# Attention, two feed-forward layers and routing in one kernel: P times v in one block, one inversion for several row sums, elu with two ScalarE passes, later transposes of gathered rows

## The chip, the cores and the metric

The kernel runs on one NeuronCore of one Trainium2 chip, as a single program. The metric is the device time of one execution in microseconds (us). Five engines take part: TensorE (PE; its weight loads are shown as PEld), VectorE (DVE), ScalarE (ACT), GpSimd (POOL) and SyncE (SP), which issues most DMAs.

## The reference

Causal attention for 4 x 12 heads over 448 positions of 64 dimensions, then a dense layer with elu on 1792 tokens of 768 values, then a layer of 8 experts, to which a greedy assignment with a capacity of 224 tokens each sends every token.

```python
scores = scale * np.matmul(q, k.transpose(0, 1, 3, 2))
scores = np.where(mask, -1e9, scores); scores -= np.max(scores, axis=-1, keepdims=True)
attn = np.exp(scores); attn = attn / (np.sum(attn, axis=-1, keepdims=True) + 1e-09)
x = np.matmul(attn, v)                     # -> [1792, 768]
h = x @ w_in                               # w_in [768, 2048]
g = np.where(h > 0.0, h, np.exp(np.minimum(h, 0.0)) - 1.0)
x2 = g @ w_out                             # w_out [2048, 768]
logits = x2 @ w_gate                       # 8 experts, greedy by sorted logit, 224 tokens each
out[mask_e] = np.maximum(x2[mask_e] @ w1[e], 0.0) @ w2[e]
```

## The kernel before

Everything is unrolled in Python. Stages are generators that emit instructions and yield the PE time that they think they used; `Sched.drive` always continues the generator that is furthest behind its weight, and `after(d, fn)` puts work of the other engines on a heap, to be emitted when the emitted PE time has moved on by `d` ns. `need(token)` empties the heap up to one item. The order on every engine is the order of emission, and each engine works through its queue strictly in that order.

Attention goes by pairs of heads, n = 0 to 23. `front(n)` makes the scores of a pair in seven blocks, i = 6 down to 0, of 64 query rows for two heads (128 partitions) and 64 (i + 1) columns: one fp32 matmul (line 200), a DVE pass that adds the mask and takes the row maximum (208), an ACT exponential with the row sum (212), and, after every second block, `recip`: add 1e-9 and invert the sums of two blocks on DVE (219, 220). `norm` then scales each block on POOL (227). Where a block's width isn't a multiple of 128, POOL zeroes the last 64 columns each time (204). `back(n)` transposes the blocks (248), ACT or DVE evacuates them into `PT` (251), and P times v runs as four chunks of key rows c = 0 to 3, each for both heads of the pair, a = 0 and 1, in the two column halves of the array (262): chunks of 448, 320, 192 and 64 columns, the last with 64 key rows. Between the chunks the generator yields, so that other generators' matmuls come in between. `att(n)` runs `front(n + 1)` and `back(n)` side by side.

For n = 0 to 5 attention runs alone; the outputs of six pairs are one batch of 448 tokens. Then batch b of the dense layer (`gemm1`: 16 column tiles m, six steps of three f32r matmuls, lines 377 to 379, with high and low parts of x and of the weights) runs beside the attention of batch b + 1. In this stage DVE also converts weights that were loaded in another format, and `fold` prepares w_out and its product with w_gate. elu of a tile stands at the end of `gemm1`: ACT takes exp of the PSUM tile (389), DVE makes min(e, 1) - 1 (390), and DVE adds max(p, 0) (393).

`gemm2` (line 629, 14 token tiles of 16 steps with six matmuls) runs beside `route`, the assignment. In its last tile the rows of expert 0 that are already in DRAM are gathered (`first_rows`: two indirect DMAs on POOL, line 663, from step 4 on), and transposed in three parts by matmuls with the identity (671) after steps 11, 12 and 13; the rows of the last tile come in by a one-hot matmul (678). The table `FIRST` says at which step how many parts are emitted. Then the experts follow one after the other.

Of the kernel before, what the change touches and what calls it, by code (L numbers as in the profile page):

```python
# [8 lines left out]
F32 = mybir.dt.float32  # L9
# [5 lines left out]
AF = mybir.ActivationFunctionType  # L15
AX = mybir.AxisListType
OP = mybir.AluOpType
# [19 lines left out]
class Sched:  # L37
# [6 lines left out]
    def after(self, d, fn):  # L44
        self.n += 1
        tok = [False]
        heapq.heappush(self.heap, (self.now + d, self.n, fn, tok))
        return tok
# [28 lines left out]
def body(ctx, tc, q, k, v, w_in, w_out, w_gate, w1, w2, out, dbg=None):  # L77
# [48 lines left out]


    KN, VN, WIN, STG = {}, {}, {}, {}

# [7 lines left out]
    def load_v(n):  # L137
        b, j = divmod(n, NP)
        VN[n] = at.tile([128, 4, 2, D], F32, name="vn", bufs=3)
        SP.dma_start(VN[n][:, 0:3], v[b, j, 0:384].rearrange("(t p) h d -> p t h d", p=128))  # L140
        SP.dma_start(VN[n][:64, 3], v[b, j, 384:])


# [49 lines left out]
    def front(n):  # L193
# [3 lines left out]
        for i in range(NQ - 1, -1, -1):  # L197
            w = 64 * (i + 1)
            p = ps.tile([128, 512], F32, name="h" if n < NP and i % 2 else "sc")
            PE.matmul(p[:, :w], qT[:, i].rearrange("p a c -> p (a c)"), kT[:, :w], start=True, stop=True)  # L200
            nb = (i + 2) // 2
            s = at.tile([128, 128 * nb], F32, name=f"s{nb}", bufs=2 if nb == 4 else 4)
            if i % 2 == 0:
                G.memset(s[:, w:w + 64], 0.0)
            t0 = 1.7 * w + 250
# [10 lines left out]

            def recip(i=i, w=w):
                j = min(i + 2, NQ)
                V.tensor_scalar_add(sm[:, 2, i:j], sm[:, 1, i:j], 1e-9)
                V.reciprocal(sm[:, 2, i:j], sm[:, 2, i:j])  # L220
                for u in range(j - 1, i - 1, -1):
                    after(400, lambda u=u: norm(u))
# [8 lines left out]
            after(t0 + 1.1 * w + 350, expo)  # L231
            if i % 2 == 0:
                after(t0 + 2.0 * w + 900, recip)
# [3 lines left out]
    def back(n):  # L237
# [21 lines left out]
        for c in range(4):  # L259
            kk = min(128, S - 128 * c)  # L260
            for a in range(2):
                PE.matmul(p[64 * a:64 * a + 64, 128 * c:S], vn[:kk, c, a, :], PT[:kk, c, a, 128 * c:],  # L262
                          start=(c == 0), stop=(c == 3), skip_group_check=True)
            yield 2 * (0.835 * (S - 128 * c) + 27)
        xs = x1 if n // NP % 2 else x0
# [99 lines left out]
    def gemm1(b):  # L365
# [3 lines left out]
        for m in range(MT):  # L369
# [18 lines left out]
            g = wk.tile([128, S], F32, name="g", bufs=5)  # L388
            after(100, lambda e=e, p=p: A.activation(e, p[:, :S], AF.Exp))
            after(700, lambda e=e: V.tensor_scalar(e, e, 1.0, -1.0, op0=OP.min, op1=OP.add))  # L390

            def fin(e=e, p=p, g=g, m=m):
                V.scalar_tensor_tensor(g, p[:, :S], 0.0, e, op0=OP.max, op1=OP.add)
                SP.dma_start(gT_d[:, m, b * S:(b + 1) * S], g)
# [55 lines left out]
    for t in qz:  # L450
        G.memset(t[64:, :, 0], 0.0)
        G.memset(t[:64, :, 1], 0.0)
    G.iota(jp, pattern=[[1, 128]], base=0, channel_multiplier=-1, allow_small_or_imprecise_dtypes=True)
    V.memset(mask, 0.0)
    V.tensor_scalar(ident, jp, 0.0, None, op0=OP.is_equal)
# [136 lines left out]
    def gemm2():  # L592
        load_g(2)
        for c in range(NT):
            p = [ps.tile([128, 512], F32, name=n) for n in ("h", "tp")]
            for m in range(MT):
                if c == 0 and m == 1:
                    yield from late()
                if c == 1 and m == 0:
                    z = gb.tile([128, DM], F32, name="x2", bufs=2)  # L600
                    V.memset(z[:1], 0.0)
                    SP.dma_start(x2_d[LAST:LAST + 1], z[:1])
                if c == NT - 1 and m == 3:
                    while 0 not in IDX:
                        yield -200
                    fg = first_rows()
                if c == NT - 1 and m in FIRST:
                    for _ in range(FIRST[m]):
                        yield next(fg)
# [34 lines left out]
            X2[0] = after(300, ev), o  # L644
        for _ in fg:
            yield 0

    X2, PX, SLOT = {}, [], {}  # L650
    FIRST = {4: 1, 12: 1, 13: 1, 14: 1}

# [392 lines left out]
```

## Time and profile before

| what | value |
|---|---|
| median of 3 runs | 1059.11 us (1058.39 to 1059.22) |
| the profiled execution | 1060.71 us, span of its instructions 1058.9 us |
| PE busy | 1027.9 us, 97% |
| DVE, ACT, POOL busy | 679.4 (64%), 440.6 (42%), 246.7 us (23%) |
| mean granted clock of PE | 0.995 |

A row of the windows view gives, for a stretch of the span, its length and the busy time and number of instructions of each engine, then the granted share of PE's clock, the DMA share and GB/s. A row of the timeline has start, duration, engine, line, operation, out<-in, shape and count of merged instructions; in brackets stands the idle time of the engine just before it and what ended it. Matmuls are pipelined, so durations overlap: the next start says how long PE was really held. A row of the groups view has the count, then busy time in us, the mean of one in ns, and the idle time before them with what ended it.

### The profile page before, as it was taken

Reading aid. Unit: us, or ns where it says so; the run is one execution under the profiler, and the core shown is the slowest. Engines: PE = TensorE matmul, PEld = TensorE weight load, DVE = VectorE, ACT = ScalarE, POOL = GpSimd, SP = SyncE. Lnnn points to the kernel's source line nnn. Section 1 sums busy time; section 2 is a strip of 40 time slices with the busy share of each in tenths; the row PEclk is TensorE's granted clock in tenths of the full one; section 3 lists DMA queues with packets and bytes.
Section 4 is the critical chain, followed back from the end, with each engine's and each line's share of the span. In section 5 each row is a group of like instructions: output and inputs, shape, how many; then the busy total and the mean of one; then the engine's idle time right before and its main releaser. Section 6 shows DMA issues by size and latency. Waiting matters only on the chain.

```text
span 1058.9 us, 17901 instructions
## 1 busy us (share of the span) xinstructions
PE 1027.9 (97%) x6615; PEld 866.4 (82%) x6615; DVE 679.4 (64%) x1691; ACT 440.6 (42%) x960; POOL 246.7 (23%) x375
## 2 busy tenths in 40 slices
PE   8999998999999999999999999999989999999997
PEld 4567776667777776887898988999989999999997
DVE  5989976786854454555766565665536766667762
ACT  5655445434444454333212111111335656556651
POOL 4356563444444443000000000000020111101110
PEclk9999999999999999999999999999999999999999
DMA  7546644665522111765333333222247786676810
GB/s 182 140 147 188 211 157 144 197 198 193 186 67 88 62 38 43 245 202 159 105 105 114 122 94 96 75 72 75 77 155 228 229 258 223 209 243 229 256 32 27
DMA packets 110857, 155.32 MB, mean 147 GB/s; under 512 B 29617, under 2 KB 82353, under 8 KB 110770
## 3 DMA queue, kind: packets, MB, share of 16 engines
q1 hardware_dynamic: 108210, 143.17, 42.9%
q0 software_dynamic: 2560, 11.01, 3.5%
q8 instruction: 52, 0.85, 0.3%
q14 instruction: 35, 0.29, 0.1%
HBM read 122.17 MB, written 31.98 MB: 146 GB/s over the span
## 4 chain that ended last, share of the span: by engine, by line
PE 80%; DVE 11%; ACT 3%; issue 3%; DMA 2%; POOL 1%; SPq 0%; POOLq 0%; DVEq 0%; ACTq 0%
PE h L629 9%; PE tp L629 8%; PE h L934 8%; PE h L377 7%; PE sc L986 6%; PE h L379 6%; PE h L378 6%; PE sc L200 5%; PE pv L262 4%; PE h L931 4%; PE pv L986 3%; PE lg L986 3%; PE tp L248 3%; PE lg L768 2%; ACT s L212 1%
## 5 line engine op out<-in xcount | busy, mean ns | idle before, releaser
L377 PE MATMUL h<-xh,wh 128*128 128x448 f32 x384 | 174.4, 454 | 0.0
L505 DVE TENSOR_TENSOR wl<-wr,wh 128x768 fp32r<-128x768 f32 x144 | 135.4, 953 | 17.5 <-ACT wh L504 17.2
L212 ACT ACTIVATE s<-s,sm 128x448 f32<-128x448 f32 (+6 forms) x168 | 85.1, 507 | 138.5 <-DVE sm L208 137.1
L379 PE MATMUL h<-xh,wl 128*128 128x448 f32 x384 | 140.7, 367 | 0.0
L378 PE MATMUL h<-xl,wh 128*128 128x448 f32 x384 | 140.3, 365 | 0.0
L504 ACT CAST wh<-wr 128x768 fp32r<-128x768 f32 x144 | 118.3, 829 | 30.2 <-PE lg L986 23.4
L227 POOL TENSOR_SCALAR s<-s,sm 128x448 f32<-128x448 f32 (+6 forms) x168 | 98.1, 596 | 111.9 <-DVE sm L220 79.3
L934 PE MATMUL h<-xt,wh 128*128 128x448 f32 x384 | 119.2, 373 | 0.0
L362 POOL TENSOR_TENSOR wl<-wr,wh 128x768 fp32r<-128x768 f32 x48 | 92.1, 1918 | 103.7 <-ACT wh L361 97.6
L639 ACT COPY x<-h 128x384 f32<-128x384 f32 x14 | 6.7, 481 | 235.7 <-PE h L629 235.7
L377 PEld LDWEIGHTS h<-xh,wh 128*128 128x128 f32 x384 | 72.5, 189 | 38.0 <-issue 29.5
L208 DVE CUSTOM_DVE_ANT_0 s<-sc,mask 128x448 f32<-128x448 f32 (+6 forms) x150 | 62.1, 420 | 63.7 <-PE sc L200 58.1
L200 PE MATMUL sc<-kT,qz 128*128 128x192 f32 (+6 forms) x300 | 92.2, 395 | 1.4 <-DVE sm L208 0.5
L931 PE MATMUL h<-xt,wl 128*128 128x224 f32 x384 | 92.1, 267 | 0.0
L629 PE MATMUL h<-wh,gh 128*128 128x384 f32 x224 | 81.5, 364 | 0.0
L378 PEld LDWEIGHTS h<-xl,wh 128*128 128x128 f32 x384 | 72.9, 190 | 8.8 <-issue 3.0
L629 PE MATMUL h<-wl,gh 128*128 128x384 f32 x224 | 77.4, 346 | 0.0
L379 PEld LDWEIGHTS h<-xh,wl 128*128 128x128 f32 x384 | 72.3, 188 | 6.1
L629 PE MATMUL h<-wh,gl 128*128 128x384 f32 x224 | 76.7, 343 | 0.0
L629 PE MATMUL tp<-wh,gl 128*128 128x384 f32 x224 | 75.5, 337 | 0.0
L629 PE MATMUL tp<-wh,gh 128*128 128x384 f32 x224 | 75.4, 336 | 0.0
L629 PE MATMUL tp<-wl,gh 128*128 128x384 f32 x224 | 75.3, 336 | 0.0
(208 smaller groups left out, 2117.5 us busy)
## 6 DMA issues: line engine op xcount, KB each, us to landing
wr<-in_moe_w_dram SPq DMA_DIRECT2D x128, 384.0 KB, 3.9
gT_d<-g SPq DMA_DIRECT2D x64, 224.0 KB, 2.0
gr<-gT_d SPq DMA_DIRECT2D x28, 512.0 KB, 3.8
st<-in_moe_w_in_dram SPq DMA_DIRECT2D x16, 767.6 KB, 4.6
st<-in_moe_w_out_dram SPq DMA_DIRECT2D x16, 767.6 KB, 4.8
wo_d<-wo SPq DMA_DIRECT2D x16, 384.0 KB, 3.0
wr<-wo_d SPq DMA_DIRECT2D x16, 384.0 KB, 3.6
qz<-in_q_dram SPq DMA_DIRECT2D x48, 112.0 KB, 3.6
```

Of the source, the lines that this page charges most:

```text
L200: PE.matmul(p[:, :w], qT[:, i].rearrange("p a c -> p (a c)"), kT[:, :w], start=True, stop=True)
L212: A.activation(s[:, :w], s[:, :w], AF.Exp, bias=sm[:, 0, i:i + 1], scale=-1.0, accum_out=sm[:, 1, i:i + 1])
L227: G.tensor_scalar(s[:, :w], s[:, :w], sm[:, 2, i:i + 1], 1.0, op0=OP.mult, op1=OP.mult)
L377: PE.matmul(p[:, :S], wh[:, c], xh, start=(c == 0), stop=False)
L378: PE.matmul(p[:, :S], wh[:, c], xl, start=False, stop=False)
L379: PE.matmul(p[:, :S], wl[:, c], xh, start=False, stop=(c == KT - 1))
L504: A.copy(wh, raw)
L505: return wh, wl, after(gap, lambda: e.tensor_sub(wl, raw, wh.bitcast(F32)))
L629: PE.matmul(p[n][:, :384], st[:, mm], wsel[:, 384 * n:384 * n + 384], start=(m == 0 and first), stop=(m == MT - 1 and st is gl))
L931: PE.matmul(p[:, :CAP], wl[:, c], xt[:, c, :CAP], start=False, stop=stop, skip_group_check=True)
L934: PE.matmul(p[:, :2 * CAP], wh[:, c], xt[:, c], start=(c == 0), stop=(c == KT - 1), skip_group_check=True)
L986: PE.matmul(acc[j][n][:HC, :384], ht[:, m, s, j * HC:(j + 1) * HC], wsel[:, 384 * n:384 * n + 384], start=(m == 0 and first), stop=(m == F ...
```

## The change

P times v: all eight matmuls of a pair are emitted before the generator yields once (1980 ns); the last chunk uses 128 key rows, with v's missing 64 rows zeroed by a POOL memset at each load. The blocks of P get tiles of their own, two for each i, whose padding is zeroed once at the start; the memset for each block goes. `recip` is called after blocks 4 and 0 only, for blocks 6 to 4 and 3 to 0. elu becomes relu(-p) on ACT, exp(-that) on ACT, and max(e - 1, p) on DVE. In `gemm2`, `FIRST` moves the three parts of the transposes: two after steps 13 and 14, the third behind the last step; the wait for the index list moves from step 3 to step 4, and the generator's own times are passed on.

```diff
+    PB = [[at.tile([128, 128 * ((i + 2) // 2)], F32, name=f"s{i}{k}", bufs=1) for k in range(2)] for i in range(NQ)]
@@ load_v
         SP.dma_start(VN[n][:64, 3], v[b, j, 384:])
+        G.memset(VN[n][64:, 3], 0.0)
@@ front
-            nb = (i + 2) // 2
-            s = at.tile([128, 128 * nb], F32, name=f"s{nb}", bufs=2 if nb == 4 else 4)
-            if i % 2 == 0:
-                G.memset(s[:, w:w + 64], 0.0)
+            s = PB[i][n % 2]
-            def recip(i=i, w=w):
-                j = min(i + 2, NQ)
+            def recip(i=i):
+                j = NQ if i else 4
                 V.tensor_scalar_add(sm[:, 2, i:j], sm[:, 1, i:j], 1e-9)
                 V.reciprocal(sm[:, 2, i:j], sm[:, 2, i:j])
-            if i % 2 == 0:
+            if i in (4, 0):
                 after(t0 + 2.0 * w + 900, recip)
@@ back
         for c in range(4):
-            kk = min(128, S - 128 * c)
             for a in range(2):
-                PE.matmul(p[64 * a:64 * a + 64, 128 * c:S], vn[:kk, c, a, :], PT[:kk, c, a, 128 * c:],
+                PE.matmul(p[64 * a:64 * a + 64, 128 * c:S], vn[:, c, a, :], PT[:, c, a, 128 * c:],
                           start=(c == 0), stop=(c == 3), skip_group_check=True)
-            yield 2 * (0.835 * (S - 128 * c) + 27)
+        yield 1980
@@ gemm1
-            after(100, lambda e=e, p=p: A.activation(e, p[:, :S], AF.Exp))
-            after(700, lambda e=e: V.tensor_scalar(e, e, 1.0, -1.0, op0=OP.min, op1=OP.add))
+            after(100, lambda e=e, p=p: A.activation(e, p[:, :S], AF.Relu, scale=-1.0))
+            after(600, lambda e=e: A.activation(e, e, AF.Exp, scale=-1.0))
             def fin(e=e, p=p, g=g, m=m):
-                V.scalar_tensor_tensor(g, p[:, :S], 0.0, e, op0=OP.max, op1=OP.add)
+                V.scalar_tensor_tensor(g, e, -1.0, p[:, :S], op0=OP.add, op1=OP.max)
@@ start
+    for i in range(0, NQ, 2):
+        for t in PB[i]:
+            G.memset(t[:, 64 * (i + 1):], 0.0)
@@ gemm2
-                if c == NT - 1 and m == 3:
-                    while 0 not in IDX:
-                        yield -200
-                    fg = first_rows()
                 if c == NT - 1 and m in FIRST:
+                    if m == 4:
+                        while 0 not in IDX:
+                            yield -200
+                        fg = first_rows()
                     for _ in range(FIRST[m]):
                         yield next(fg)
@@ after the last tile
-        for _ in fg:
-            yield 0
+        for c in fg:
+            yield c
-    FIRST = {4: 1, 12: 1, 13: 1, 14: 1}
+    FIRST = {4: 1, 14: 1, 15: 1}
```

## Rows read from the trace of the kernel before

**Rows 1.** Windows of three attention stages: busy time and count of each engine, clock.
```profile
15.20:66.00 50.80, 47.25 (x268) 27.38 (x268) 39.67 (x163) 33.73 (x108) 24.23 (x64) 1.00 0.55 140
66.00:315.00 249.00, 239.66 (x1444) 176.20 (x1442) 192.80 (x500) 115.43 (x303) 122.22 (x159) 0.99 0.53 172
315.00:435.00 120.00, 120.00 (x659) 89.02 (x658) 57.13 (x181) 55.20 (x135) 47.20 (x74) 1.00 0.21 67
```

**Rows 2.** Timeline of PE in the fused stage: line, operation, tiles, shape, count.
```profile
300.94 0.60 PE L248 MATMUL tp<-ident,s 128*128 128x128 f32 x4
301.47 0.63 PE L313 MATMUL tp<-woT,wg 128*32 128x128 f32 x12
...
302.34 0.36 PE L378 MATMUL h<-xl,wh 128*128 128x448 f32 x1
302.54 0.37 PE L379 MATMUL h<-xh,wl 128*128 128x448 f32 x1
...
304.01 0.81 PE L200 MATMUL sc<-kT,qz 128*128 128x384 f32 x2
...
304.86 0.37 PE L378 MATMUL h<-xl,wh 128*128 128x448 f32 x1
```

**Rows 3.** Timeline of PE: first run of line 262, one run, the last run.
```profile
15.22 0.97 PE L262 MATMUL pv<-pt,vn 128*64 128x448 f32 x4
...
311.40 0.37 PE L379 MATMUL h<-xh,wl 128*128 128x448 f32 x1
311.70 0.97 PE L262 MATMUL pv<-pt,vn 128*64 128x448 f32 x4
...
312.92 0.36 PE L378 MATMUL h<-xl,wh 128*128 128x448 f32 x1
...
423.38 0.33 PE L262 MATMUL pv<-pt,vn 64*64 64x64 f32 x4
```

**Rows 4.** Timeline of PE: chunks of 192 and 64 columns in one run.
```profile
249.08 0.81 PE L262 MATMUL pv<-pt,vn 128*64 128x192 f32 x8
...
250.13 0.36 PE L378 MATMUL h<-xl,wh 128*128 128x448 f32 x1
```

**Rows 5.** Groups of instructions: sums, reciprocals and exponentials of the softmax.
```profile
L212 ACT ACTIVATE s<-s,sm 128x448 f32<-128x448 f32 (+6 forms) x168 | 85.1, 507 | 138.5 <-DVE sm L208 137.1
L219 DVE TENSOR_SCALAR sm<-sm 128x1 f32<-128x1 f32 (+1 forms) x96 | 23.4, 243 | 21.4 <-ACT s L212 21.4
L220 DVE RECIPROCAL sm<-sm 128x1 f32<-128x1 f32 (+1 forms) x96 | 15.9, 165 | 3.3
```

**Rows 6.** Timeline of PE in the first stage: last score block, later transposes.
```profile
26.21 0.33 PE L200 MATMUL sc<-kT,qz 128*128 128x64 f32 x2
...
30.49 0.82 PE L248 MATMUL tp<-ident,s 128*128 128x128 f32 x6
```

**Rows 7.** Timeline of POOL in the same stretch: four scalings in a row.
```profile
27.41 1.69 POOL L227 TENSOR_SCALAR s<-s,sm 128x256 f32<-128x256 f32 x4 [0.89 <-ACT s L212]
```

**Rows 8.** Groups: all transposes of P and what they waited for.
```profile
L248 PE MATMUL tp<-ident,s 128*128 128x128 f32 x384 | 60.3, 274 | 7.5 <-ACT pt L251 4.2 <-DVE pt L251 3.0
```

**Rows 9.** Groups: the first two passes of elu.
```profile
L389 ACT ACTIVATE e<-h 128x448 f32<-128x448 f32 x64 | 34.7, 542 | 68.1 <-PE h L379 68.1
L390 DVE TENSOR_SCALAR e<-e 128x448 f32<-128x448 f32 x64 | 31.3, 490 | 38.1 <-ACT e L389 37.6
```

**Rows 10.** Timeline of ACT: the only table load of the trace.
```profile
0.73 1.28 ACT L212 ACT_TABLE_LOAD   x1 [0.73 <-PEq L1033]
```

**Rows 11.** Timeline of PE at the end of gemm2: gathered rows, then one-hot matmuls.
```profile
775.44 0.47 PE L671 MATMUL sc<-ident,gr 112*128 112x112 f32 x2 [1.88 <-DMA gr<-x_d,i]
776.40 0.92 PE L671 MATMUL sc<-ident,gr 112*128 112x112 f32 x6 [0.48 <-DMA gr<-x_d,i]
...
785.33 1.78 PE L678 MATMUL sc<-oh,x 128*128 128x224 f32 x8 [0.44 <-ACT x L639]
```

**Rows 12.** Windows: the stretch after that gap, columns as in the first group.
```profile
777.80:781.20 3.40, 3.40 (x15) 3.40 (x14) 0.00 (x0) 0.00 (x0) 0.00 (x0) 0.50 0.00 0
```

## The prediction

> **What bounds the kernel now.** I read the table of windows first, one row for each stage of the first half [rows 1]. TensorE (PE) is busy 120.0 of 120 us in the last attention stage, 239.7 of 249 in the one before it and 47.3 of 50.8 at the start; DVE is the next (192.8 of 249), and ACT (115) and POOL (122) have half their time free. So time is won by making PE's own stream shorter, and what is taken off DVE, ACT or POOL counts only through the 9.3 + 3.6 us in which PE stood still. Busy is not the same as working, and so the second view is PE's timeline, start against start, and not the durations, which overlap.
>
> Plain gemm1 matmuls (448 columns, f32r) start 0.20 us apart: 302.34, 302.54 [rows 2]. A score block of 384 columns in fp32 (two records) takes 304.01 to 304.86, less 0.20 for the L377 in between: 0.65, that is 1.68 ns a column or 0.84 a pass, and nothing is lost in going in or out. Now a run of P times v (line 262): from L379 at 311.40 to L378 at 312.92 are 1.52; the two f32r matmuls in it take 0.41, the 448 columns 0.75 (both heads run side by side in the two column halves of the array) [rows 3]. So **0.36 us is spent on entering and leaving the narrow shape**. The timeline has 86 such unbroken runs of line 262, the first at 15.22 and the last at 423.38 [rows 3]. I use 0.35, the figure of the other widths too.
>
> **P times v as one block.** All eight matmuls of a pair of heads are now issued before the generator yields, so nothing can come between: 24 runs instead of 86, 62 removed. What does going from one chunk to the next cost inside a run? The nearest row with the same shape throughout is L313: six 32-column matmuls in two rounds. From 300.94 to 302.34 are 1.40; less 0.20 for L377, 0.43 for four transposes (128 x 0.84 ns each) and 0.43 for the two rounds of two passes, 0.34 is left, as much as for a run of one round: the second round is free [rows 2]. The other end is the place where chunks of 192 and 64 columns already stand together, but in two shapes (128 rows, then 64): 249.08 to 250.13 are 1.05, less 0.20 and 0.43 (256 columns) leaves 0.42, where the 448 run, counted from its own start, leaves 1.22 - 0.20 - 0.75 = 0.27. So that join costs 0.15 [rows 3, 4]. The change gives the last chunk 128 rows too (zeros in v's padding), so all four chunks have one shape; I take the L313 row: 0. The ten joins there are now (six in the first stage, four later) vanish as well.
>
> The Trainium skill says otherwise: "TensorE: Matmul & The Clock Gate", Part 3, has weight loads overlap with running matmuls only where the row group differs, and here every chunk uses all rows. By that each of three boundaries would cost about what the join costs now; the L313 row, where all rounds also use all 128 rows, speaks against it.
>
> Fused stage (18 pairs, 68 runs to 18): 50 x 0.35 + 4 x 0.15 = **18.1 us**. First stage (6 pairs, 18 runs to 6): 12 x 0.35 + 6 x 0.15 = 5.1 us at most.
>
> **Batched inversion.** Two instead of four pairs of tiny DVE operations for each pair of heads: 48 x (0.243 + 0.165) = 19.6 us less on DVE [rows 5], worth nothing by itself where PE is full. What it costs is delay: blocks 3 to 0 are scaled only when block 0's exponential is done. In the first stage block 0's scores start at 26.21 and end 0.3 later; the transposes of blocks 2 and 3 start at 30.49, 4.0 later [rows 6]. The last run of P times v (some 0.75: 0.43 for 256 columns and most of a run's 0.35) stood in between and now lies ahead, so 3.3 are left. In the new order the last three score blocks follow one another, so three exponentials (0.51 each [rows 5]) stand in line: 1.5, then sum and reciprocal 0.41, then POOL, whose four scalings took 1.69 in a row [rows 7], some 1.1 of it, by width, for the first two: 3.0, and 3.6 for all four against 3.3 + 0.43. That is a margin of 0.1 to 0.3 us, and a DVE conversion pass in front eats it. Bounds: nothing is lost, or all 5.1. I take half: **2.5 us** gained. Once, at the very start, block 6 waits for block 4's exponential: 0 to two ACT passes (1.0); I take **-0.5**.
>
> In the fused stage gemm1 lies between these steps, and no transpose there waits for POOL: the idle time before the line 248 transposes (7.5 us in all) is 7.2 us of waiting for evacuations by ACT and DVE [rows 8]. Nothing is charged.
>
> **Memsets.** 96 small ones leave POOL's queue, 24 (v's padding) and 8 (once) come in. The one for v waits for P times v of three pairs earlier at its buffer; the scalings queued behind it on POOL need scores that PE computes after that. Covered by POOL's idle half [rows 1]; without that cover it costs no more than the 96 cost now. 0.
>
> **elu.** A DVE pass (0.490) becomes an ACT pass; the nearest row is the present one from PSUM, 0.542 [rows 9]. 64 x 0.49 = 31 us leave DVE, 35 us come to ACT, which has them free. The chain from the last matmul to g grows by 0.05; two h buffers cover it. Evacuations and casts queued behind it on ACT come up to 0.5 later, as those on DVE come 0.5 earlier. Relu and Exp need no table swap: the whole trace has one load, at 0.73 [rows 10], though line 947 runs Relu after line 389's Exp. On the path it could cost 64 x 0.05 = 3.3 us or win some of PE's stalls; I take 0, both ends in the range. The Trainium skill ("ScalarE: Activation LUTs", Rules for kernel authors) sends relu to VectorE; that rule is about the pass alone, 0.05 here, and would make 3 us more where ACT were the bound.
>
> **Transposes of the gathered rows.** The gathers are issued at the same step as before. PE stands 1.88 us before the first transposes (775.44) and 0.48 before the next (776.40) [rows 11]. Two steps are 12 matmuls of 384 columns, 0.175 each by the f32r spacing, 2.1 us: the first wait goes, about 0.4 of the second stays: **1.9**. After this gap the granted clock is 0.50 from 777.80 to 781.20 [rows 12] (1.2 instead of 2.4 GHz): half of 3.4 us, **1.7**, goes with it, since the first stage, with 3.6 us of short stalls in all, keeps a clock of 1.00 [rows 1]. The last third of the transposes now stands behind the last gemm2 matmul, where PE waits 0.44 for the copy of x (785.33) [rows 11]: **0.4**. Next late is the second gather. Waiting for the index list at step 4 and not 3 changes nothing: PE shows no stop there. Together **4.0 us** (1.9 to 4.4).
>
> **Sum.** 18.1 + 2.5 - 0.5 + 4.0 + 0 = 24.1 us. The profiled execution took 1060.7 (span 1058.9): 1036.6. The median of the runs is 1.6 lower, 1059.1: **1035.0 us**.
>
> **Rivals.**
> 1. Each chunk boundary costs 0.15 although the shape is the same: 24 x 3 x 0.15 = 10.8 us less, **1045.8**. For it: the join of today [rows 4]. Against: L313 [rows 2]. 0.10. The Trainium skill's rule on weight loads, above, would lead here.
> 2. Between 66 and 315 us conversions on DVE, their DMA loads and the fold set the pace, and a faster PE only waits more. Of the 50 removed runs about 30 lie there: 10.5 us are not gained, **1045.5**. For it: 9.3 us of stalls are there now [rows 1]. Against: DVE loses its share of the 51 us, so its 77% do not rise. 0.13.
> 3. The relief of DVE takes half of these stalls with it and the first stage loses nothing: 4.7 + 2.5 less, about **1028**; all of them, 1023. 0.15.
> 4. Slower than before: the four scalings of blocks 3 to 0, now issued together and late, hold PE at the transposes of blocks 2 and 3 in every fused step, for as long as they take in a row: 18 x 1.69 = 30 us [rows 7], **1065**. It decides from 24.1 / 18 = 1.3 us a pair. Against: no wait for POOL shows at these transposes now [rows 8], and gemm1's matmuls stand between. 0.04.
> 5. The joined block changes nothing, because the 0.35 is paid at each chunk anyway, and the waits for the gather only move: 1059. 0.04.
>
> **How the numbers follow.** The forecast (1029 to 1041) has 0.54. The range takes in rivals 1 and 2 and the middle of rival 3: 1026 to 1046; outside lie rivals 4 and 5 and the ends of the others, somewhat under 2 in 10. Within 0.2% (2.1 us, about what a measurement of this kernel can tell from no change) needs rival 5, 0.04; slower needs rival 4, 0.04; faster is all the rest, 0.92.
>
> **What would show it.** In PE's timeline of the new kernel: 24 runs of line 262's matmuls of 16 records, each about 2.07 us of PE time (1024 columns at 1.68 ns, and 0.35 of shape); 2.5 would be rival 1. In the first stage some waits of the transposes for POOL. In the windows, PE stalls of 66 to 315 us near 9; 15 and more would be rival 2, under 5 rival 3. At the end of gemm2 one gap of about 0.4 us and the clock at 1.00. What would make all of it wrong is a new wait in the fused stage that returns with every pair.

## The result and the profile after

The changed kernel takes 1048.49 us (median of four executions, 1047.79 to 1051.09) against 1059.02 us for the kernel before beside it: a ratio of 0.9906, with a 95% interval of 0.9889 to 0.9923. It is faster by 10.5 us, where the prediction said 24.1. Its profiled execution took 1051.09 us (span 1049.3), the longest of the four; the shares below come from it.

The windows of the same three stretches as in [rows 1], and one over the end of gemm2 (length, then PE, PEld, DVE, ACT and POOL busy, granted clock, DMA share, GB/s):

```profile
15.20:66.00 50.80, 43.35 (x262) 27.36 (x260) 36.79 (x133) 31.83 (x100) 23.19 (x45) 1.00 0.51 131
66.00:315.00 249.00, 236.92 (x1473) 184.29 (x1473) 174.05 (x434) 132.25 (x343) 112.97 (x130) 0.99 0.54 173
315.00:435.00 120.00, 118.54 (x673) 94.14 (x673) 46.64 (x145) 65.25 (x160) 45.62 (x57) 1.00 0.25 83
760.00:790.00 30.00, 29.50 (x183) 28.20 (x182) 16.27 (x26) 13.96 (x26) 8.63 (x5) 1.00 0.69 220
```

PE now stands still in all three: 7.5 us of the first (3.6 before), 12.1 of the second (9.3) and 1.5 of the third (0 before). That is where the missing gain has gone. To place it, I took from PE's timeline the moments at which the four batches' gemm1, gemm2 and the experts begin. The last two lines of this table are worked out from the same timeline: of each stretch between two trios of gemm1 matmuls, the time from start to start, less the work in it by the spacings of the prediction, is split into 0.35 for each entry into a narrow shape ("shape") and the rest ("waits"). The idle time in brackets alone is too small a measure, as an example below shows.

| us | before | after | before + block (e2) | after without block (e15) | after + doubled chunk (e17) |
|---|---|---|---|---|---|
| start to gemm1 of batch 0 | 63.5 | 66.9 | 64.7 | 64.1 | 65.0 |
| gemm1 of batch 0 to batch 1 | 111.6 | 107.7 | 110.3 | 108.4 | 112.0 |
| batch 1 to 2 | 142.4 | 141.1 | 144.2 | 140.8 | 143.8 |
| batch 2 to 3 | 108.1 | 104.7 | 104.0 | 108.5 | 109.1 |
| batch 3 to gemm2 | 69.1 | 69.5 | 69.1 | 69.6 | 69.7 |
| gemm2 to experts | 292.9 | 288.2 | 294.0 | 287.9 | 293.0 |
| fused steps: shape | 36.2 | 19.4 | 19.4 | 36.2 | 19.4 |
| fused steps: waits | 15.2 | 22.9 | 27.8 | 11.0 | 21.3 |

A lower clock counts among the waits here. In the fused steps the traces of before and after have 3.4 us at a granted clock of 0.50, of which half, 1.7 us, is lost; e2 has 10.2 such us (5.1 lost), e15 none, e17 3.4 (1.7). The middle step, batch 1 to 2, of e2 and of e15 (the clock is the third number from the end):

```profile
175.10:319.20 144.10, 135.97 (x910) 103.48 (x909) 100.52 (x270) 63.84 (x175) 58.25 (x88) 0.96 0.53 174
172.50:313.30 140.80, 135.89 (x911) 99.21 (x909) 90.14 (x229) 71.84 (x187) 54.16 (x58) 1.00 0.55 178
```

From before to after the three fused steps win 8.6 us (16.8 of shape less 7.7 of waits; 0.5 isn't placed), the gather 4.7, and the time up to gemm1 grows by 3.4, the step from batch 3 to gemm2 by 0.4: 9.5 of the 9.6 us between the spans.

**The block itself** does what was forecast. One run in PE's timeline of after:

```profile
328.05 0.37 PE L379 MATMUL h<-xh,wl 128*128 128x448 f32 x1
328.35 1.95 PE L262 MATMUL pv<-pt,vn 128*64 128x448 f32 x16
330.23 0.47 PE L377 MATMUL h<-xh,wh 128*128 128x448 f32 x1
330.54 0.36 PE L378 MATMUL h<-xl,wh 128*128 128x448 f32 x1
```

Read it as [rows 3] was read: from L379 to L378 are 2.49, less 0.40 for two gemm1 matmuls: 2.09, of which 1.72 are the 1024 columns and 0.37 the shape. There are 24 such runs where there were 86.

**The gather** too. PE after the change at the end of gemm2, where [rows 11] had 1.88, 0.48 and 0.44:

```profile
770.36 0.47 PE L675 MATMUL sc<-ident,gr 112*128 112x112 f32 x2
771.20 0.92 PE L675 MATMUL sc<-ident,gr 112*128 112x112 f32 x6 [0.37 <-DMA gr<-x_d,i]
...
775.84 1.69 PE L682 MATMUL sc<-oh,x 128*128 128x224 f32 x8
```

One gap of 0.37 is left, and the clock, 0.50 in [rows 12], is 1.00 in the window from 760 to 790.

**The first stage** got longer, but by less than the 3.4 us of the table. Of these, 1.9 stand ahead of the first run of P times v, which starts at 17.12 where [rows 3] has 15.22:

```profile
7.84 1.49 PE L204 MATMUL h<-kT,qz 128*128 128x384 f32 x2
9.12 1.11 PE L204 MATMUL sc<-kT,qz 128*128 128x320 f32 x2
...
17.12 1.95 PE L262 MATMUL pv<-pt,vn 128*64 128x448 f32 x16
```

The 384 columns hold PE for 1.28 us, start to start, and not for the 0.65 of [rows 2]: this execution began at half speed. The change isn't the reason. The profiled execution of e1 below, whose first stage is that of before, begins in the same way (first run at 17.08), and those of e13 and e17, whose first stage is that of after, don't (15.39 and 15.15). From the first run of P times v to gemm1 pass 48.3 us in before, e1 and e3, and 49.8 to 49.9 in after, e13 and e17: the change costs 1.5 us there.

PE, and POOL and DVE below it, at the counterpart of [rows 6, 7]:

```profile
25.25 1.95 PE L262 MATMUL pv<-pt,vn 128*64 128x448 f32 x16
...
27.78 0.33 PE L204 MATMUL sc<-kT,qz 128*128 128x64 f32 x2
28.30 1.02 PE L204 MATMUL sc<-kT,qz 128*128 128x448 f32 x2 [0.18 <-DVE sm L209]
...
30.60 0.52 PE L249 MATMUL tp<-ident,s 128*128 128x128 f32 x3 [0.51 <-ACT pt L252]
...
32.46 1.08 PE L249 MATMUL tp<-ident,s 128*128 128x128 f32 x6 [0.69 <-POOL s L228]
```

```profile
30.83 2.21 POOL L228 TENSOR_SCALAR s<-s,sm 128x256 f32<-128x256 f32 x4 [1.77 <-DVE sm L221]
```

```profile
31.00 1.11 DVE L174 CUSTOM_DVE_ANT_0 cq<-st,cv 128x768 int32<-128x768 int8 x1
```

Block 0's scores end near 28.1 (27.78 and the 0.3 that the prediction used). POOL gets the inverted sums at 30.83, 2.7 later, and PE has the first two scaled blocks at 32.46, 1.6 after that: a chain of 4.4 where I had added up 3.0. The sum stood in DVE's order behind a row maximum of the next pair (29.73 to 30.33), and block 2's scaling took 1.12 of POOL's 1.6 us, beside the conversion pass on DVE; it took 1.12 beside such a pass in two more of the six pairs, and 0.42 or 0.43 in the other three. PE runs out of other work before, waits 0.69 for POOL, and the pairs from here to 66 us each show such waits (the POOL one 0.60 to 0.69).

**The fused steps.** Groups of PE instructions from 63 to 425 us, before and then after (count, busy, mean ns, idle time ahead of them and its releasers):

```profile
L200 PE MATMUL sc<-kT,qz 128*128 128x448 f32 (+6 forms) x238 | 72.1, 391 | 0.5 <-DVE sm L208 0.5
L248 PE MATMUL tp<-ident,s 128*128 128x128 f32 x288 | 45.8, 273 | 4.0 <-DVE pt L251 2.2 <-ACT pt L251 1.8
```

```profile
L204 PE MATMUL sc<-kT,qz 128*128 128x256 f32 (+6 forms) x245 | 72.9, 390 | 3.9 <-DVE sm L209 3.6
L249 PE MATMUL tp<-ident,s 128*128 128x128 f32 x288 | 46.8, 275 | 5.9 <-POOL s L228 2.9 <-ACT pt L252 2.1 <-DVE pt L252 0.8
```

The score blocks, which hardly ever waited, now wait for DVE's row maxima. PE and DVE of after at one such place, in the last fused step, where DVE converts no weights:

```profile
350.71 0.49 PE L204 MATMUL sc<-kT,qz 128*128 128x192 f32 x2
...
351.65 0.39 PE L204 MATMUL sc<-kT,qz 128*128 128x128 f32 x2
352.43 0.44 PE L204 MATMUL sc<-kT,qz 128*128 128x64 f32 x2 [0.40 <-DVE sm L209]
...
353.38 0.92 PE L204 MATMUL sc<-kT,qz 128*128 128x448 f32 x2
```

```profile
351.48 0.62 DVE L394 SCALAR_TENSOR_TENSOR g<-e,h 128x448 f32<-128x448 f32 x1 [4.89 <-ACT e L391]
352.02 0.35 DVE L209 CUSTOM_DVE_ANT_0 s<-sc,mask 128x192 f32<-128x192 f32 x1
```

The third small block needs the PSUM buffer of the first, whose row maximum DVE begins only at 352.02, behind elu's last step. The idle time says 0.40, but the 128-column block started 0.78 earlier and holds PE 0.22 (128 columns at 1.68 ns): 0.56 are lost.

### The profile page after: what moved, and what is told of

It is laid out like the page before. It is cut to its first block, busy times and chain, and to the rows that moved or that the text cites. A ratio compares the mean times of both kernels' runs of the same rounds, so it can differ in the third digit from the quotient of the medians.

```text
span 1049.3 us, 17726 instructions
## 1 busy us (share of the span) xinstructions
PE 1012.6 (97%) x6615; PEld 874.3 (83%) x6615; DVE 638.1 (61%) x1531; ACT 469.1 (45%) x1024; POOL 234.4 (22%) x311
## 4 chain that ended last, share of the span: by engine, by line
PE 81%; DVE 8%; ACT 3%; DMA 3%; issue 2%; POOL 2%; SPq 0%; POOLq 0%; DVEq 0%; ACTq 0%
PE h L633 9%; PE tp L633 8%; PE h L938 8%; PE h L377 7%; PE sc L990 6%; PE h L379 6%; PE h L378 6%; PE sc L204 5%; PE pv L262 4%; PE h L935 4%; PE tp L249 3%; PE pv L990 3%; PE lg L990 3%; PE lg L772 2%; DMA st<-in_moe_w_out_dram 1%
## 5 line engine op out<-in xcount | busy, mean ns | idle before, releaser
L377 PE MATMUL h<-xh,wh 128*128 128x448 f32 x384 | 170.8, 445 | 0.0
L379 PE MATMUL h<-xh,wl 128*128 128x448 f32 x384 | 140.9, 367 | 0.0
L378 PE MATMUL h<-xl,wh 128*128 128x448 f32 x384 | 140.7, 366 | 0.0
L228 POOL TENSOR_SCALAR s<-s,sm 128x448 f32<-128x448 f32 (+6 forms) x168 | 90.2, 554 | 116.2 <-DVE sm L221 105.1
L394 DVE SCALAR_TENSOR_TENSOR g<-e,h 128x448 f32<-128x448 f32 x64 | 39.6, 619 | 88.2 <-ACT e L391 88.1
L378 PEld LDWEIGHTS h<-xl,wh 128*128 128x128 f32 x384 | 72.9, 190 | 9.4 <-issue 3.2
L379 PEld LDWEIGHTS h<-xh,wl 128*128 128x128 f32 x384 | 72.4, 188 | 6.7 <-POOL wl L362 0.6
## 6 DMA issues: line engine op xcount, KB each, us to landing
qz<-in_q_dram SPq DMA_DIRECT2D x48, 112.0 KB, 3.3
```

Of the source, the lines that this page charges most:

```text
L228: G.tensor_scalar(s[:, :w], s[:, :w], sm[:, 2, i:i + 1], 1.0, op0=OP.mult, op1=OP.mult)
L377: PE.matmul(p[:, :S], wh[:, c], xh, start=(c == 0), stop=False)
L378: PE.matmul(p[:, :S], wh[:, c], xl, start=False, stop=False)
L379: PE.matmul(p[:, :S], wl[:, c], xh, start=False, stop=(c == KT - 1))
```

## The experiments

Each was timed beside the kernel before on the same chip (1058.4 to 1058.7 us). Medians are of four to ten executions, the ratio to before has its 95% interval behind it, and stages and waits are those of one profiled execution of each.

### One part at a time, put into the kernel before

Each of these is the kernel before with the lines of one part of the change's diff, which stands above: e1 those of `gemm2`, `FIRST` and the last tile, e2 those of `back` and `load_v`, e3 those of `gemm1`, e4 those of `recip`. In short:

```diff
e1_gather
+    FIRST = {4: 1, 14: 1, 15: 1}
e2_block
-            yield 2 * (0.835 * (S - 128 * c) + 27)
+        yield 1980
e3_elu
+            after(600, lambda e=e: A.activation(e, e, AF.Exp, scale=-1.0))
e4_batch
+            if i in (4, 0):
```

> The kernel before with the later transposes of the gathered rows alone. Working of the prediction: 4.0 us less (waits of 1.88 and 0.44 gone, half-clock stretch of 3.4 us gone), about 1055. Comparing the traces of before and after gives 4.8 us less from the first gemm2 matmul to the experts (293.2 to 288.5): 1054.3. If part of that came from elsewhere: 1056 or more.

> The kernel before with P times v as one block alone (last chunk with 128 rows, v's padding zeroed; inversion in pairs, elu and gather as before). Theory A (the block now stands ahead of the last three score blocks, which then come back to back behind two PSUM buffers and reach the softmax late; the wait of PE for row maxima comes from that): 16.9 us of shape saved, about half lost, 1047 to 1051. Theory B (the losses come from the batched inversion): nearly the whole 20 us, 1037 to 1041. Theory C (DVE conversions and the fold set the pace whatever is done to PE): 1048 to 1052 with stalls in the stretch with conversions only, none after 320 us.

> The kernel before with elu in two ACT passes and one DVE pass alone. Prediction: 0, with 3.3 us more and some 5 less as ends. Theory C (DVE sets the pace between 66 and 315 us): 3 to 8 us less, since 31 us leave DVE. If ACT's queue matters more: 2 to 5 us more.

> The kernel before with the batched inversion alone (blocks 6 to 4 and 3 to 0). Theory B: 5 to 10 us more, most of it before 66 us, where the transposes then wait for POOL. Theory A: within 3 us of before, as the last score blocks still stand apart from each other. If the 20 us taken off DVE count: 2 to 5 us less.

| run | median us | ratio to before | waits in the fused steps |
|---|---|---|---|
| e1_gather | 1055.39 | 0.9966 (0.9951 to 0.9982) | 12.8 |
| e2_block | 1056.09 | 0.9977 (0.9963 to 0.9990) | 27.8 |
| e3_elu | 1061.73 | 1.0036 (1.0025 to 1.0046) | 17.4 |
| e4_batch | 1057.25 | 0.9989 (0.9976 to 1.0001) | 10.5 |

The block alone saves its 16.8 us of shape and gives 12.6 back in waits, 3.4 of them by the clock (5.1 us lost to it against 1.7), in a profiled execution of 1059.45 us, 3.4 above the median. Its 1056.09 lies outside the ranges of all three theories. The batched inversion by itself does the fused steps no harm: their waits fall from 15.2 to 10.5, or from 13.5 with the clock left out (e1 and e4 lose nothing to it there, e3 1.7). elu alone is slower by 3.4 us, which I had put at nothing. The four differences add up to -3.0 us where together they are -10.5, so the parts don't simply add.

### The first stage and the size of the last chunk

e5 puts the block behind the next pair's first transposes again, e6 inverts the sums in pairs again, e7 does both, e8 gives the last chunk back its 64 key rows.

```diff
e5_late
-        yield -1000
+        yield -2400
e6_pairs
-                j = NQ if i else 4
+                j = min(i + 2, NQ)
-            if i in (4, 0):
+            if i % 2 == 0:
e7_late_pairs: both
e8_k64
-                PE.matmul(p[64 * a:64 * a + 64, 128 * c:S], vn[:, c, a, :], ...
+                PE.matmul(p[64 * a:64 * a + 64, 128 * c:S], vn[:kk, c, a, :], ...
```

(e5 and e7 also raise the weight of those generators from 45000 to 53100.)

> The changed kernel with one difference: the generator paces itself by 2400 and not 1000 before the block (the batch's weight in the outer pacing raised from 45000 to 53100 to keep it), so that P times v stands behind the last three score blocks and not ahead of them. Theory A (the new waits come from the place of the block, ahead of scores that PE then needs results of): waits of scores for row maxima gone, stalls of the fused stages down from 23 to about 15 us, 4 to 5 us less before the first gemm1 matmul: 1035 to 1040. Theory A' (2 us of P times v without other matmuls starve DVE and ACT wherever the block stands): 1046 to 1050. Theory C (DVE conversions): 1046 to 1050, with stalls between 100 and 290 us.

> The changed kernel with the inversion in pairs again. By the run with the batch alone (1.1 us less): 1049 to 1051. Theory B (batched inversion is what holds the transposes): 1036 to 1042.

> The changed kernel with the block behind the last three score blocks and the inversion in pairs. Theory A: as the run with the late block, up to 2 us more, 1036 to 1042. Theory B: 1034 to 1036. Theory A': 1046 to 1051.

> The changed kernel with 64 rows in the last chunk, in one block. If a change of the rows inside a block costs 0.15 us, as the join of 192 and 64 columns before: a run of line 262 longer by 0.15, 24 x 0.15 = 3.6 us more where PE is full, 1050 to 1052. If a boundary costs nothing in any shape: 1048.5.

| run | median us | ratio to before | start to gemm1 of batch 0 | waits in the fused steps |
|---|---|---|---|---|
| after | 1048.49 | 0.9906 (0.9889 to 0.9923) | 66.9 | 22.9 |
| e5_late | 1052.62 | 0.9947 (0.9927 to 0.9966) | 63.1 | 26.7 |
| e6_pairs | 1051.99 | 0.9935 (0.9913 to 0.9958) | 64.4 | 27.3 |
| e7_late_pairs | 1052.52 | 0.9939 (0.9919 to 0.9960) | 61.2 | 27.8 |
| e8_k64 | 1053.64 | 0.9954 (0.9935 to 0.9973) | 67.4 | 24.2 |

Up to gemm1 e5 is 3.8 us shorter than after, e6 2.5 and e7 5.7, but 1.9 of each is the half-speed start of after's profiled execution. That leaves 1.9 for the late block, 0.6 for the pairs and 3.8 for both, which is 2.3 better than before (0.8 of it an earlier first score block, at 5.29 and not 6.12): the two edits together are the loss there. In the fused steps neither helps; both make the waits longer, by 2 to 4 us if what the clock takes is left out (3.4 us in e5 and e7, 1.7 in e6 and after). Theory A, which had 1035 to 1042 for a late block, fails. e8's run of P times v:

```profile
328.70 0.37 PE L380 MATMUL h<-xh,wl 128*128 128x448 f32 x1
329.00 2.10 PE L263 MATMUL pv<-pt,vn 128*64 128x448 f32 x16
331.02 0.47 PE L378 MATMUL h<-xh,wh 128*128 128x448 f32 x1
331.33 0.36 PE L379 MATMUL h<-xl,wh 128*128 128x448 f32 x1
```

That is 2.63 from L380 to L379 where after has 2.49: the switch to 64 rows costs 0.14, as the join in [rows 4] did, and boundaries without a switch cost nothing. (e8's 24.2 us of waits hold 18 x 0.14 = 2.5 of it.) By the medians e8 is 5.1 us slower than after, where 24 x 0.14 is 3.4; its profiled execution has 6.8 us at a clock of 0.50 in the first stage, which after's hasn't.

### elu, and a first stage in the old order

e9 is after with elu as before; e10 emits elu's last step on DVE 0.8 us later; e11 adds e7's edits to e10 for the first six pairs alone; e12 is e9 with the same.

```diff
e10_fin
-            tok = after(1100, fin)
+            tok = after(1900, fin)
e11_fin_first: that, and
-        yield -1000
+        yield -2400 if n < 6 else -1000
-                j = NQ if i else 4
+                j = min(i + 2, NQ) if n < 6 else NQ if i else 4
-            if i in (4, 0):
+            if i in (4, 0) or n < 6 and i % 2 == 0:
e9_noelu, e12_noelu_first: the first two passes
-            after(100, lambda e=e, p=p: A.activation(e, p[:, :S], AF.Relu, scale=-1.0))
+            after(100, lambda e=e, p=p: A.activation(e, p[:, :S], AF.Exp))
```

> The changed kernel with elu as before (one ACT pass, two DVE passes). Theory D (the third step of elu, due 1100 ns after the tile, reaches DVE's queue before ACT has done two passes, and row maxima and evacuations queued behind it wait; DVE idle ahead of line 394: 88 us): 1043 to 1046, with the stage of the third batch (104.7 us) 1 to 2 us shorter. If the 31 us less on DVE are what the block needs (additive in the other sense): 1050 to 1053.

> The changed kernel with the third step of elu due at 1900 and not 1100 ns, nothing else. Theory D: DVE's idle time ahead of that step falls from 88 us to under 45, waits of scores for row maxima get fewer, the third batch's stage goes from 104.7 to about 103, total 1043 to 1046. Theory A' (PE's lump of 2 us alone): 1048 to 1050.

> As the run before, and in the first stage (pairs 0 to 5) the block behind the last score blocks and the inversion in pairs, whose effect there was 66.9 to 61.2 us in the run with both: 5 us less than the run before, 1038 to 1041.

> elu as before, and in the first stage the block behind the last score blocks and the inversion in pairs: 5 us less than the run with elu as before alone. If gains add up: 1038 to 1041.

Measured: e9 1049.59 us (0.9918, 0.9895 to 0.9940), e10 1050.13 (0.9921, 0.9899 to 0.9943), e11 1046.64 (0.9886, 0.9864 to 0.9908), e12 1048.96 (0.9908, 0.9886 to 0.9930). The elu passes of after, and its last step in e10:

```profile
L390 ACT ACTIVATE e<-h 128x448 f32<-128x448 f32 x64 | 34.7, 542 | 68.7 <-PE h L379 68.5
L391 ACT ACTIVATE e<-e 128x448 f32<-128x448 f32 x64 | 37.0, 578 | 0.8
L394 DVE SCALAR_TENSOR_TENSOR g<-e,h 128x448 f32<-128x448 f32 x64 | 39.6, 619 | 88.2 <-ACT e L391 88.1
```

```profile
L394 DVE SCALAR_TENSOR_TENSOR g<-e,h 128x448 f32<-128x448 f32 x64 | 39.5, 617 | 39.1 <-ACT e L391 39.0
```

In [rows 9] DVE waited 37.6 us for ACT at its first elu step; in after it is 88.1, with row maxima queued behind, as at 351.48 above. e10 halves this and the time doesn't fall: the idea that DVE, held up at elu, makes PE's waits is wrong as the main cause. With the block in the kernel, the old elu and the new one can't be told apart (1049.6 and 1048.5). The first stage in the old order is worth 2.9 us by the profiles of e10 and e11 (65.7 and 62.8) and 3.5 by their medians, but only 0.6 by the medians of e9 and e12; the 5 us that were expected, and 1038 to 1041, came in neither. e11, at 1046.64, has the lowest median of all; its interval and that of after overlap, so that it beats after isn't shown.

### Single waits taken away

The longest wait of the fused steps in after, and who works around it:

```profile
229.41 0.52 PE L249 MATMUL tp<-ident,s 128*128 128x128 f32 x3 [2.87 <-POOL s L228]
```

```profile
224.66 2.05 POOL L362 TENSOR_TENSOR wl<-wr,wh 128x768 fp32r<-128x768 f32 x1 [7.33 <-ACT wh L361]
```

```profile
225.29 1.45 DVE L220 TENSOR_SCALAR sm<-sm 128x4 f32<-128x4 f32 x1 [0.25 <-ACT s L213]
```

```profile
228.03 0.67 ACT L213 ACTIVATE s<-s,sm 128x448 f32<-128x448 f32 x1 [2.36 <-DVE sm L209]
...
228.70 0.56 ACT L252 COPY pt<-tp 128x512 f32<-128x512 f32 x1
```

The sum on DVE, four columns, takes 1.45 us and ends at 226.74; POOL's subtraction ends at 226.71. Then the row maximum of the next pair's block 6 follows, its exponential on ACT at 228.03, and only behind that, in ACT's order, the evacuation that PE needs. (The bracket names POOL, whose last scaling ended at 229.34; but the block that is transposed at 229.41 had been scaled at 215.9, and in the trace PE's queue is held for ACT, whose copy ended at 229.26.) e13 emits that exponential 2 us later, e14 moves POOL's subtraction to DVE, e16 gives one set of transposes a PSUM buffer of its own. e18 is the text of e13 a second time, in spite of its label.

```diff
e13_exp6, e18_exp6_first
-            after(t0 + 1.1 * w + 350, expo)
+            after(t0 + 1.1 * w + (2350 if i == 6 and n > 6 else 350), expo)
e14_wlv
-    (V if b == 3 else G).tensor_sub(wl, ...
+    V.tensor_sub(wl, ...
e16_tp3
+    p = ps.tile([128, nb, 2, ni, 64], F32, name="lg", bufs=1) if ii == (5,) and n < 12 else ...
```

> The changed kernel with one order changed: in the fused stage the exponential of block 6 is due 2000 ns later, so that on ACT it stands behind the evacuation of the previous pair's first transposes and not ahead of it. Theory G (PE's waits at the transposes come through ACT's queue: evacuation behind that exponential, exponential behind DVE's row maximum): the waits of transposes for ACT and the one of 2.9 us at 229.4 go, 4 to 7 us less: 1041 to 1045. Theory H (waits only move on to the next thing that is late): 1047 to 1050.

> Placeholder combination is not used: this is the changed kernel with the exponential of block 6 emitted 2.0 us later in the fused stage, as in the run e13, repeated to learn how far two builds of one text differ. Both theories: 1047.2 within 1.5 us.

> The changed kernel with the 48 subtractions that make the low parts of w_in on DVE (0.95 us each) and not on POOL (1.9 us). Theory F (POOL's subtraction holds up small DVE operations, as the sum of 1.45 instead of 0.15 us at 225.3): sums and conversions take their short times, the fused stages lose 3 to 6 us of stalls: 1043 to 1046. If DVE's load is what counts (46 us more on it): 1052 to 1060.

> The changed kernel with a third PSUM buffer for the transposes of block 5 of pairs 0 to 11 (one that is free until the second batch). Theory G: the 0.5 us wait of the third transposes goes from each pair of the first stage (3 us) and the waits for evacuation from the first batch's stage (2 us): 1043 to 1045. Theory H: waits move to the scalings by POOL and to the evacuations for P times v: 1047 to 1049.

Measured: e13 1047.18 us (0.9887, 0.9862 to 0.9912) and its repeat 1048.60 (0.9907, 0.9891 to 0.9924), e14 1050.95 (0.9926, 0.9900 to 0.9951), e16 1050.33 (0.9920, 0.9896 to 0.9944). None differs from after by more than the intervals allow. Each edit worked on what it was aimed at: in e14 the mean of that small DVE operation falls from 252 to 167 ns and the long wait from 2.87 to 2.12 us, in e13 it falls to 1.79; in e13 and e16 the transposes' waits for ACT in the fused steps fall from 2.1 to 0.2 and 0.6 us. But the score blocks' waits for row maxima grow from 3.6 to 5.5, 5.9 and 5.8 us in e13, e14 and e16. The waits move; none of these three queues alone is their cause.

### The block out again, and time added to it

e15 is after with P times v in four runs as before. e17 is after with the first chunk of the block issued twice in the fused steps; the second issue writes over the first.

```diff
e15_noblock
-        yield 1980
+            yield 2 * (0.835 * (S - 128 * c) + 27)
e17_twice
-        for c in range(4):
+        for c in ([0, 0, 1, 2, 3] if n > 5 else range(4)):
```

> The changed kernel with P times v in four runs as before (inversion, elu and gather stay changed). If the parts add up (gather 3.0, batch 1.1, elu -3.4 us): 1056 to 1058, the block being worth 8 to 10 us in this company, though 2.3 alone. If the block is worth 2.3 here too: 1050 to 1051.

> The changed kernel, but in the fused stage (pairs 6 to 23) the first chunk of P times v, 448 columns for both heads, is issued twice in a row; the second issue writes over the first, so the output stays the same. That adds 448 columns x 1.68 ns = 0.75 us to the PE stream in each of 18 pairs, 13.5 us, with no other instruction changed. Theory S (slack: PE has so little reserve over its in-order partners that about half of any time taken out of the stream comes back as waits, whatever the shape of the block): adding 13.5 gives back about half of it as shorter waits, the waits of PE in the three fused steps fall from 23 us towards 16, and the median rises from 1048.5 to about 1055. Theory O (order: it is the unbroken block, which sends the transposes and score blocks of one pair close together, that makes the waits): the waits stay near 23 us or grow, and the median rises by the whole 13.5, to 1062.

e15 took 1052.36 us (0.9935, 0.9910 to 0.9959; the interval overlaps that of after), e17 1062.15 (1.0031, 1.0019 to 1.0043). Score blocks at the place in the pair where after had its 0.40, first e15, then e17:

```profile
346.77 0.49 PE L203 MATMUL sc<-kT,qz 128*128 128x192 f32 x2
...
349.20 0.55 PE L203 MATMUL sc<-kT,qz 128*128 128x128 f32 x4
...
351.81 0.91 PE L203 MATMUL sc<-kT,qz 128*128 128x448 f32 x2
```

```profile
357.28 0.49 PE L204 MATMUL sc<-kT,qz 128*128 128x192 f32 x2
...
358.21 0.38 PE L204 MATMUL sc<-kT,qz 128*128 128x128 f32 x2
359.01 0.44 PE L204 MATMUL sc<-kT,qz 128*128 128x64 f32 x2 [0.42 <-DVE sm L209]
...
359.95 0.92 PE L204 MATMUL sc<-kT,qz 128*128 128x448 f32 x2
```

With four runs, the last three score blocks and the next pair's first are spread over 5.0 us, two runs of P times v (three chunks) between them; with the block they stand within 2.7. The groups of e15 and of e17 from 63 to 425 us say the same for all pairs:

```profile
L203 PE MATMUL sc<-kT,qz 128*128 128x448 f32 (+6 forms) x238 | 72.1, 391 | 0.1
L248 PE MATMUL tp<-ident,s 128*128 128x128 f32 x288 | 45.9, 274 | 2.1 <-ACT pt L251 2.0 <-DVE pt L251 0.2
```

```profile
L204 PE MATMUL sc<-kT,qz 128*128 128x192 f32 (+6 forms) x244 | 72.3, 390 | 3.4 <-DVE sm L209 3.2
L249 PE MATMUL tp<-ident,s 128*128 128x128 f32 x288 | 46.9, 276 | 6.2 <-POOL s L228 2.9 <-ACT pt L252 2.4 <-DVE pt L252 0.8
```

e17 adds 18 x 0.75 = 13.5 us inside the block. Had PE merely lost reserve by getting faster, about half of that would have been taken up by shorter waits. They fall by 1.6 (22.9 to 21.3), the wait for the row maxima at this place stays at 0.4, the fused steps get 11.4 longer and the median 13.7. (The second part of those 13.7 isn't clean: in e17's profiled execution the wait for the gathered rows is back with 1.94 us and the clock drop behind it, 4.8 us in all, which after doesn't have.) e15 and e17 spend nearly the same time on PE (36.2 us of shape against 19.4 + 13.5 = 32.9, beside the same work) and yet wait 11.0 and 21.3. So it is the order and not the speed: time inside the block covers nothing, since the waits stand elsewhere in the pair.

## Why the prediction was right and where it was wrong

- **Shape of P times v: right.** 2.07 us a run forecast, 2.09 measured. For the fused steps 18.1 were forecast; 16.8 is what 48 fewer entries into a narrow shape at 0.35 make, since two of the 50 removed runs stood beside other narrow matmuls. Boundaries between chunks of one shape cost nothing, so rival 1 falls, and with it the rule of the Trainium skill ("TensorE: Matmul & The Clock Gate", Part 3) as I had applied it: e8 pays 0.14, for a switch in the number of rows.
- **The fused steps: wrong, and the largest miss.** The step that failed is the one sentence "Nothing is charged", and before it the sum that multiplied 50 removed runs by 0.35 as if the chunks did nothing but compute. 7.7 us came back as waits (the clock takes 1.7 of them before and after alike). I read the idle time ahead of the transposes [rows 8] as if it would stay, though it had been measured with the chunks in between. They also kept score blocks and transposes apart, so that DVE, ACT and POOL, each in its order, were in time. e2 against before (waits 15.2 to 27.8, or 13.5 to 22.7 without the clock) and e15 against after (11.0 and 22.9, or 11.0 and 21.2) show that the block makes the waits; e17 shows that it isn't lost reserve. With the other parts in place the block is worth 3.9 us by the medians (1052.36 to 1048.49, with intervals that overlap), and 4.2 by the fused steps of the profiles.
- **Rival 2** gave a time near the result (1045.5), by another mechanism: it made DVE's conversions the pace. But the last fused step, where DVE converts nothing, gives back 2.9 of 6.2 us too, and e15, with the same conversions, has few waits. PE's idle time from 66 to 315 is 12.1, between the 9 of the forecast and the 15 of that rival. **Rival 3** falls as a whole, though its relief exists: e4 and e15 wait 4 to 5 us less than before in the fused steps, 2.5 to 3 without the clock, and with the block this is gone. **Rival 4** had the right kind (a new wait in every pair) and the wrong place: not the four scalings, but above all the row maxima, and about 8 us more waits in all, not 30.
- **First stage: wrong in sign.** 2.5 - 0.5 = +2.0 forecast, -1.5 measured (from the first run of P times v on; the other 1.9 of the table's 3.4 is a half-speed start that e1 has too). The 0.5 at the very start doesn't show: the first run stands at 15.39 and 15.15 in e13 and e17, at 15.22 before. The terms that were mis-sized: exponentials, sum and inversion took 2.7 us from the last score block and not 1.9, with the sum behind another pair's row maximum, and POOL's first two scalings 1.6 and not 1.1 (four: 2.21, not the 1.69 of [rows 7]) beside the DVE conversion pass that I had named and not priced. My margin of 0.1 to 0.3 us was worked out from best cases; I had "all 5.1" lost as a bound, but no loss beyond it. e7 shows that about 1.5 us of gain was there with the late block and the pairs.
- **Gather: right.** 4.0 forecast, 4.7 in the profile, 3.0 alone (e1). e17 shows how thin it is: there the gathers land a median of 9.1 us after issue, in after 7.3, with loads of expert weights (384 KB each, on SP's queue) in the same stretch in both; why they took longer isn't shown.
- **elu at 0: right in company, wrong alone.** In the changed kernel it can't be told from nothing (e9), in the kernel before it costs 3.4 us (e3), the 3.3 of my bound. Which wait makes these 3.4 I didn't settle.
- **Memsets at 0:** nothing in the runs speaks against it; not tried by itself.

Open: that the score blocks can be spread again with the block left whole, by the weight of their generator, wasn't tried. So it isn't separated whether the waits come from score blocks and transposes that stand close together or from the 2 us in which the block gives DVE and ACT nothing new; that e17 makes the block 0.75 longer and the waits don't grow speaks for the first. Nor is it known why e6 and e7 lengthen the fused waits.

## What to carry to other kernels

On a full TensorE, pieces that pay a shape cost can also be the spacing that keeps in-order engines in time; before joining them, write down which two instructions each piece stands between, and what the second one waits for. Price a joined block by what is left adjacent, not by the idle time measured while the pieces were in between. To learn whether returned waits come from speed or from order, add the saved time back inside the block: if the waits stay, it is the order. And before a stage of one profile is compared with another's, look at the same stage in other runs that share its text: here a half-speed start stood for over half of a 3.4 us loss.

## What the runs showed of the hardware

A DVE operation on four columns took 1.45 us while POOL subtracted two SBUF tiles, ending 0.03 us after it; its mean over the kernel fell from 252 to 167 ns in e14, which has no such subtractions on POOL. The Trainium skill ("SBUF — State Buffer", SBUF: two separate sides) gives DVE and GpSimd one shared port pair, an exclusive lock that one of them holds for a whole instruction, where the DVE operation is in a two-port mode or, beside a GpSimd operation that reads SBUF, has two SBUF inputs. The times above are what such a lock would give; whether this sum is in such a mode no run here shows.

The step from batch 1 to 2 took 142.6 us in e13 and 139.5 in e18, whose text is the same, at a mean clock of 0.98 and 1.00. Part of such differences is the clock behind one long wait. In e2, near the place where after waits 2.87 us and goes on at a clock of 1.00 (229.4 to 234), PE waits 2.97 and then runs at 0.50, the lower of the two levels (1.2 GHz):

```profile
228.06 0.88 PE L249 MATMUL tp<-ident,s 128*128 128x128 f32 x3 [2.97 <-ACT pt L252]
```

```profile
228.00:233.00 5.00, 4.94 (x26) 3.93 (x27) 2.17 (x7) 0.86 (x3) 0.79 (x1) 0.50 0.72 239
```

Half of these 5 us is what the drop takes on top of the wait. The length of the wait alone doesn't say whether it comes: in e14 PE goes on at 0.50 after 2.12 us at this place (225.7 to 229.0). Near 48 us PE waits 1.88 us in e9, e10, e17 and e18 and 1.89 in e13; in e9, e10 and e18 it then has 3.4 us at 0.50, in e13 and e17 none.
